# A fused adaLN, dilated-attention and token-MLP kernel: folding a modulation into weights, moving transposes and sums between engines, and issuing in a new order

## The chip, the cores and the metric

The kernel runs on one core of one Trainium2 chip. The metric is device time in microseconds (us) of one execution; less is better. The profiled execution is a little shorter than a timed one, because its span runs only from the first to the last instruction: 225.9 us of span go with 227.8 us of time.

The engines are TensorE (PE in the profile; PEld is its weight load), VectorE (DVE), ScalarE (ACT), GpSimd (POOL) and SyncE (SP; SPq is its queue, which issues nearly all DMAs in order). PSUM is where TensorE writes its results.

## The reference, cut to what matters

```python
# x: (1, 2048, 512); 32 heads of 16; window of 8 keys, dilation 2; MLP of width 1792 over the tokens
mod = silu(c) @ w_mod                       # sa, ca, ga, sb, cb, gb: six rows of 512
h = layernorm(x) * (1 + ca) + sa            # "first modulation"
q, k, v = split(h @ wqkv)
x = x + ga * (dilated_local_attention(q, k, v) @ wo)
h = layernorm(x) * (1 + cb) + sb
h3 = layernorm(h)                           # h3: 2048 tokens x 512
u = gelu(einsum('sd,sf->df', h3, w1) + b1)  # MLP 1 sums over all 2048 tokens
y = einsum('df,fs->ds', u, w2) + b2         # MLP 2
x = x + gb * y.T
```

## The kernel before

The 16 tiles of 128 tokens are worked in five chunks of 2, 4, 4, 4 and 2 tiles. For each chunk: layernorm, transpose, QKV, windowed attention, output projection, two more layernorms to h3. MLP 1 needs all tokens; it is summed in three levels (tiles 0 to 5, 6 to 9, 10 to 15). Between levels the partial sums are "parked" in SBUF as `gT`, and TensorE injects them into the next level's PSUM accumulation with an identity matmul.

Every operation is handed to a small planner in the kernel. It holds a duration for each operation, a rank (RANK, by kind of operation) and a bias between VectorE and ScalarE (BIAS), lays the operations out in time greedily, and thereby fixes both the engine and the order in which each engine gets its instructions. On the chip this order is static.

```python
RANK = {'st1': -69.27, 'ln1': -327.95, 'tr': -152.8, ...}       # order constants
BIAS = {'n1': 1.63, 'hT': 2.81, 'ev': 1.88, ...}
... POOLN1=(3, 5, 7, 8, 11),      # tiles whose first norm runs on GpSimd
    LN2D=(2, 3, 10, 11, 12, 14, 15),  # tiles whose statistics run on VectorE
    NPRE=5,                       # MLP-1 accumulators of the last level begun early
    XDMA=(1, 2, 3, 4),            # chunks transposed by DMA
...
if ch in XDMA:
    for sl, st in enumerate(tiles):
        ... nc.sync.dma_start_transpose(out=hT[:, :, sl * P:(sl + 1) * P], in_=h3[:, st, :])
    for kt in range(KT):          # then the first modulation, in place
        ... tensor_scalar / activation(h_, h_, scale=a1col[:, kt], bias=sacol[:, kt])
else:                             # chunk 0: TensorE transposes, modulation on eviction from PSUM
    ...
# QKV: lhsT = w_r[t][:, kt, j::4], rhs = hT[:, kt, :]
...
# shifted V for the attention: 16 DMAs per chunk on the same queue
dma(dst, v_c[dhi::4, :, s0:s0 + C + 8], ..., f"vd{ch}_{dhi}{w4}")
...
if li > 0:                        # MLP 1: inject the parked sums
    nc.tensor.matmul(ps(s_), lhsT=ident[:], rhs=gT[:, ft, :], start=True, stop=False)
...
if last:
    nc.scalar.activation(gT[:, ft, :], ps(s_), ACT.Gelu_apprx_tanh, bias=b1col[:, ft:ft + 1])
```

## Time and profile before

| | before |
|---|---|
| time, median of 4 runs | 227.83 us (227.06 to 228.93) |
| span of the profiled run | 225.9 us |
| first 512-column QKV matmul (chunk 1) | 35.5 us |
| last h3 tile ready | 158.1 us |
| first MLP-2 matmul | 174.0 us |

The last three rows are milestones. The last h3 tile is the end of the last VectorE `h<-h,rs,nb` instruction (two merged at 157.41, 0.73 us long). Between it and MLP 2 lies the tail of MLP 1, which needs that tile.

Busy time by stretch, kernel before. The columns are the stretch and its length, busy us (and instructions) of PE, PEld, DVE, ACT and POOL, the granted TensorE clock, the DMA share and GB/s.

```profile
8.00:20.00 12.00, 10.14 (x63) 6.99 (x61) 7.04 (x14) 7.33 (x15) 2.22 (x1) 0.72 1.10 312
20.00:46.00 26.00, 16.66 (x124) 6.72 (x125) 17.74 (x30) 14.95 (x28) 5.64 (x5) 0.80 0.76 151
46.00:98.00 52.00, 49.90 (x403) 23.34 (x410) 49.35 (x47) 47.46 (x106) 0.00 (x0) 1.00 0.90 160
98.00:158.00 60.00, 59.63 (x422) 26.15 (x428) 57.43 (x104) 48.40 (x112) 0.00 (x0) 1.00 0.89 200
158.00:174.00 16.00, 15.89 (x74) 7.28 (x75) 0.15 (x1) 8.98 (x14) 0.00 (x0) 1.00 0.41 109
```

From 46 to 158 us TensorE and VectorE are both over 95% busy. From 20 to 46 us neither is, and the clock is at 0.80. From 158 to 174 us VectorE has almost nothing to do, ScalarE is busy for 9 us, and TensorE is full.

Why the start-up is slow shows in the DMA queue's timeline (start, us, what) of the kernel before:

```profile
18.69 1.30 SPq L191 DMA_TRANSPOSE hT<-h  x1
...
21.59 5.13 SPq L191 DMA_DIRECT2D vD<-v_c  x6
26.82 3.86 SPq L191 DMA_TRANSPOSE hT<-h  x3
30.72 2.56 SPq L191 DMA_DIRECT2D vD<-v_c  x4
```

The four transposes of chunk 1 (one, then three) stand in one queue with the V loads of chunk 0. The issue of the last one ends at 30.7 us; ScalarE modulates from 32.4 us on, and the first QKV matmul of chunk 1 starts at 35.54 us.

```profile
35.54 1.90 PE L191 MATMUL psS<-hT,w_qkv 128*128 128x512 bf16 x4
```

Two groups of the kernel before that the change touches (line, engine, operation, count, then busy us and mean ns, then idle time before them and what ended it):

```profile
L191 DVE TENSOR_TENSOR big<-a2sb,vD 128x4096 bf16<-128x4096 bf16 (+1 forms) x20 | 36.9, 1860 | 6.9 <-DMA vD<-v_c 6.7
...
L191 PE MATMUL psS<-gT,ident 128*128 128x512 bf16 x28 | 10.6, 380 | 0.0
```

VectorE loses 6.7 us waiting for V loads; TensorE makes 28 injection matmuls, of which 14 are in the last level.

### The profile page before, as it was taken

How to read it: one execution, taken by the hardware profiler on the slowest of the kernel's cores; microseconds unless marked ns; L12 is line 12 of the kernel's file. 1: busy time of each engine (PE TensorE's matmuls, PEld its weight loads, DVE VectorE, ACT ScalarE, POOL GpSimd, SP SyncE). 2: the span in 40 equal slices, each digit the busy share in tenths (PEclk: the TensorE clock that was granted, in tenths of full speed). 3: DMA queues.
4: the chain of work that ended last, by engine and by line, in shares of the span. 5: the costliest groups of instructions: out<-in, count | busy, mean ns of one | idle time of the engine just before them, and what ended most of it. 6: DMA issues, size and time to landing. Idle time of an engine off the chain costs nothing.

```text
span 225.9 us, 3720 instructions
## 1 busy us (share of the span) xinstructions
PE 205.7 (91%) x1380; PEld 98.5 (44%) x1402; DVE 157.9 (70%) x236; ACT 131.2 (58%) x279; POOL 11.6 (5%) x35
## 2 busy tenths in 40 slices
PE   7596647879999999989999999999999999999993
PEld 6473212334534543735344333444444444444453
DVE  3278874598998989999999998998000344555444
ACT  3646476487979999999897957984744000000000
POOL 6008140000000000000000000000000000000000
PEclk9769885999999999999999999999999999999999
DMA  6999963496999499499998484896255511011111
GB/s 191 353 311 312 177 114 93 105 340 180 142 140 138 104 150 144 101 206 166 173 216 226 115 222 150 246 303 178 73 150 150 129 46 48 25 46 46 49 46 49
DMA packets 55302, 34.76 MB, mean 154 GB/s; under 512 B 20596, under 2 KB 54772, under 8 KB 55284
## 3 DMA queue, kind: packets, MB, share of 16 engines
q1 hardware_dynamic: 55276, 34.52, 68.8%
q8 instruction: 11, 0.18, 0.4%
q14 instruction: 7, 0.06, 0.1%
q10 hardware_dynamic: 8, 0.00, 0.0%
HBM read 22.03 MB, written 2.10 MB: 107 GB/s over the span
## 4 chain that ended last, share of the span: by engine, by line
PE 61%; DMA 12%; SPq 9%; ACT 8%; DVE 6%; issue 3%; DVEq 0%; ACTq 0%
PE psS L191 58%; SPq L191 9%; DMA gT<-in_w_mod_dram 5%; DVE big L191 5%; DMA vD<-v_c 5%; PE psL L191 2%; ACT hT L191 2%; DMA hT<-h 2%; ACT h L191 2%; ACT xx L191 1%; ACT junk L191 1%; ACT v_c L191 1%; ACT a2sb L191 1%; DVE m L191 1%; DVE st L191 1%
## 5 line engine op out<-in xcount | busy, mean ns | idle before, releaser
L191 PE MATMUL psS<-h,wst 128*128 128x512 bf16 x216 | 53.2, 379 | 0.4
L191 PE MATMUL psS<-hT,w_qkv 128*128 128x512 bf16 (+1 forms) x235 | 50.2, 363 | 1.3 <-ACT hT L191 0.7
L191 PEld LDWEIGHTS <-wst 128*128 128x128 bf16 x308 | 29.7, 98 | 33.1 <-issue 1.5
L191 PEld LDWEIGHTS <-w_qkv 128*128 128x128 bf16 x282 | 31.1, 116 | 27.8 <-issue 9.3
L191 DVE TENSOR_TENSOR big<-a2sb,vD 128x4096 bf16<-128x4096 bf16 (+1 forms) x20 | 36.9, 1860 | 6.9 <-DMA vD<-v_c 6.7
L191 DVE SCALAR_TENSOR_TENSOR h<-psS,bcol,gb_bc 128x512 f32<-128x512 f32 (+1 forms) x17 | 12.2, 719 | 41.3 <-PE psS L191 41.3
L191 DVE TENSOR_TENSOR big<-q_sb,k_c 128x4096 bf16<-128x4096 bf16 (+1 forms) x20 | 36.8, 1857 | 0.5 <-PE psL L191 0.5
L191 DVE BATCH_NORM_STATS2 st<-xx 128x6 f32<-128x512 bf16 x23 | 15.6, 677 | 7.9 <-DMA xx<-in_A_x_dram 7.2
L191 ACT ACTIVATE h<-xx,nb,rs 128x512 bf16<-128x512 bf16 x26 | 19.9, 804 | 0.2 <-DVE nb L191 0.2
L191 PE MATMUL psS<-gT,big 128*128 128x512 bf16 x82 | 18.2, 379 | 0.1
L191 PE MATMUL psS<-woq,o_sb 128*128 128x512 bf16 x60 | 16.3, 380 | 1.2 <-ACT o_sb L191 0.9
L191 PE MATMUL psS<-big,stack 128*32 128x512 bf16 (+1 forms) x160 | 11.0, 354 | 6.4 <-DVE big L191 6.3
L191 PE MATMUL psS<-gT,wst 128*128 128x512 bf16 (+1 forms) x83 | 15.3, 343 | 0.1
L191 PEld LDWEIGHTS <-ident 128*128 128x128 bf16 (+1 forms) x121 | 10.4, 113 | 9.4 <-issue 2.2
L191 PEld LDWEIGHTS <-big 128*128 128x128 bf16 x116 | 9.2, 97 | 11.4 <-DMA big<-in_w_mod_dram 1.2
L191 ACT ACTIVATE gT<-psS,bcol 128x512 bf16<-128x512 f32 x14 | 9.2, 688 | 7.2 <-PE psS L191 7.2
L191 ACT ACTIVATE hT<-hT,sacol,a1col 128x512 bf16<-128x512 bf16 (+1 forms) x16 | 11.1, 756 | 2.9 <-DMA hT<-h 2.9
L191 ACT ACTIVATE k_c<-psS 128x512 bf16<-128x512 f32 x16 | 9.5, 596 | 4.6 <-PE psS L191 4.6
L191 DVE TENSOR_TENSOR h<-h,xx 128x512 bf16<-128x512 f32 (+1 forms) x17 | 11.2, 661 | 0.6
L191 ACT ACTIVATE q_sb<-psS 128x512 bf16<-128x512 f32 x16 | 9.5, 595 | 3.6 <-PE psS L191 3.4
L191 ACT ACTIVATE gT<-psS 128x512 bf16<-128x512 f32 x19 | 10.5, 594 | 1.5 <-PE psS L191 1.4
L191 DVE BATCH_NORM_STATS2 st<-h 128x6 f32<-128x512 bf16 x16 | 10.8, 672 | 0.0
(89 smaller groups left out, 212.2 us busy)
## 6 DMA issues: line engine op xcount, KB each, us to landing
vD<-v_c SPq DMA_DIRECT2D x48, 130.0 KB, 5.2
wst<-in_B_w_dram SPq DMA_DIRECT2D x6, 768.0 KB, 5.0
wst<-in_B_w_dram SPq DMA_DIRECT2D x4, 896.0 KB, 5.5
big<-in_B_w_dram SPq DMA_DIRECT2D x3, 896.0 KB, 5.3
vD<-v_c SPq DMA_DIRECT2D x32, 66.0 KB, 3.3
out_dram<-h SPq DMA_DIRECT2D x15, 128.0 KB, 1.7
w_qkv<-in_A_wqkv_dram SPq DMA_DIRECT2D x3, 512.0 KB, 6.7
xx<-in_A_x_dram SPq DMA_DIRECT2D x3, 512.0 KB, 7.1
```

The source lines that it names most:

```text
L191: r = fn(*a, **k)
```

## The change

The intent, in four parts:

1. **Folding.** `(norm * (1+ca) + sa) @ W` equals `norm @ ((1+ca) * W) + sa @ W`. The weights are scaled once (12 pieces of 128x512), `sa @ W` becomes a bias added when q and v are evicted (for k it cancels in the softmax), and the 20 modulations of the transposed activations go.
2. **Chunk 1 transposed by TensorE** instead of DMA.
3. **The last level's parked sums added by VectorE** into PSUM instead of injected by TensorE; and six instead of five early accumulators (NPRE).
4. **A new issue order**: new RANK and BIAS, other tiles on GpSimd and VectorE, other durations in the planner; and *fillers*, idle identity matmuls that the planner puts into TensorE gaps longer than 0.45 us before 48 us of its plan, to keep the clock up.

The diff, cut to its core:

```diff
-RANK = {'st1': -69.27, 'ln1': -327.95, ...}      # 19 ranks, 11 biases
+RANK = {'st1': -24.42, 'ln1': -184.6, ...}       # all new
-    NPRE=5,
+    NPRE=6,
-    POOLN1=(3, 5, 7, 8, 11),
-    LN2D=(2, 3, 10, 11, 12, 14, 15),
-    GRP=(2, 2, 4, 1, 2),
-    XDMA=(1, 2, 3, 4),
+    POOLN1=(2, 3, 4, 10, 11, 12, 13),
+    LN2D=(2, 3, 10, 11, 12, 13, 14, 15),
+    GRP=(2, 2, 4, 1, 1),
+    XDMA=(2, 3, 4),
+    INJ=(1,),
+    VPOOL=(2, 3),
+    FILL=48.0,
...
+    def scale_w(t):
+        for kt in range(KT):
+            ... w_r[t][:, kt, :] = wraw[t][:, kt, :] * a1col[:, kt]   # VectorE or ScalarE; two on GpSimd
+    # qvb[:, t] = sa @ W for q and v, 16 one-column matmuls each
...
-            for kt in range(KT):
-                ... hT = hT * a1col + sacol
...
+            # q, v: eviction adds qvb as a bias
...
+            if e == "pe" and 0.0 < eng_free.get(e, 0.0) < self.FILL and r - eng_free[e] > 0.45:
+                ... order.append(self.filler(t0_, n_, k_[1]))
...
+                    add("dve", 0.69, lambda ft=ft, s_=s_: nc.vector.tensor_tensor(
+                        ps(s_), ps(s_), gT[:, ft, :], op=ALU.add), reads=[("gT", ft)], writes=[s_], ...)
```

More of the change, by code (lines that the diff above doesn't have):

```diff
@@ L89, in add_any, with filler @@
         return op
+    def filler(self, t, n, k):
+        f = _Op(-1, [("pe", n * 0.06, lambda: self.fill_fn(k, n))], 0.0, "filler", 0, 0.0)
+        f.start, f.end = t, t + n * 0.06
+        f.alloc = f.frees = f.behind = None
+        return f
     def schedule(self):
@@ L107, in pick @@
             return min(((max(f[k], f[k + 1]), k) for k in f if k % 2 == 0 and k + 1 in f), default=None)
+        dep_ready = {}
         def ready_time(o, e):
-            r = 0.0
-            if o.alloc is not None and o.alloc.i is None:
-                r = pick(o.alloc)[0] + self.XLAT
-            for d in o.deps:
-                od = ops[d]
-                if od is o.behind or od.eng == e == "pe":
-                    t = od.start + od.dur
-                else:
-                    t = od.end + self.XLAT
-                if t > r:
-                    r = t
+            r = dep_ready.get((o.idx, e))
+            if r is None:
+                r = 0.0
+                for d in o.deps:
+                    od = ops[d]
+                    if od is o.behind or od.eng == e == "pe":
+                        t = od.start + od.dur
+                    else:
+                        t = od.end + self.XLAT
+                    if t > r:
+                        r = t
+                dep_ready[o.idx, e] = r
+            if o.alloc is not None and o.alloc.i is None:
+                r = max(r, pick(o.alloc)[0] + self.XLAT)
             if o.bytes_:
@@ L148, in schedule @@
             o.start = r
+            if e == "pe" and 0.0 < eng_free.get(e, 0.0) < self.FILL and r - eng_free[e] > 0.45:
+                t0_ = eng_free[e]
+                n_ = int((r - t0_ - 0.25) / 0.06)
+                k_ = min(((f, k) for k, f in free["ps"].items()), default=(1e9, None))
+                if k_[0] + 0.2 < t0_:
+                    order.append(self.filler(t0_, n_, k_[1]))
             if o.alloc is not None:
@@ L237, in _t_mm @@
     return n * (cols / 2400.0 + 0.004)
-RANK = {'st1': -69.27, 'ln1': -327.95, 'tr': -152.8, 'qk_w': 51.55, 'v_w': 88.32, 'vd': 56.52, 'qk': 54.4,
-        'sm': -280.01, 'pv': 119.44, 'wo': 286.24, 'ln2': 35.59, 'aff': 123.88, 'ln3': 64.65, 'mod': 49.12,
-        'ld_x2': -99.25, 'ld_mod': -9.58, 'mlp': 1048.65, 'pre': 3000.0, 'last': 5000.0}
-BIAS = {'n1': 1.63, 'hT': 2.81, 'ev': 1.88, 'halo': 2.21, 'a2': 1.96, 'oev': 0.57, 'x1': 1.99, 'n2': 3.01,
-        'n3': -0.23, 'park': -0.82, 'row': 2.4}
+RANK = {'st1': -24.42, 'ln1': -184.6, 'tr': -140.25, 'qk_w': 53.91, 'v_w': 78.53, 'vd': 149.45, 'qk': 108.09,
+        'sm': -342.67, 'pv': 129.78, 'wo': 334.17, 'ln2': -35.94, 'aff': 219.78, 'ln3': 15.39, 'mod': -61.06,
+        'ld_x2': -184.29, 'ld_mod': -33.96, 'mlp': 904.99, 'pre': 2857.66, 'last': 5184.17}
+BIAS = {'wsc': -0.09, 'n1': 5.48, 'hT': 3.91, 'ev': 3.07, 'halo': 3.23, 'a2': 1.6, 'oev': 1.69, 'x1': 6.58,
+        'n2': 4.08, 'n3': -0.4, 'park': -1.13, 'row': 0.54}
 @with_exitstack
@@ L280 @@
     G.WIN = WIN
+    G.FILL = FILL
     R = dict(RANK, **(R or {}))
@@ L342 @@
     onecol = T([P, 1], F32, "onecol")
-    sacol = T([P, KT], F32, "sacol")
     a1col = T([P, KT], F32, "a1col")
@@ L351 @@
     ecol = T([P, KT], F32, "ecol")
+    sab = T([P, KT], BF, "sab")
+    qvb = T([P, 2, 4], F32, "qvb")
     c_t = T([KT, P], BF, "c_t")
@@ L368, in copy2, with dma @@
                          bias=bias, frees=frees)
-    def dma(out_ap, in_ap, nbytes, reads, writes, name, rate=345e3, **kw):
-        return add("sp", 0.6, lambda: nc.sync.dma_start(*(a() if callable(a) else a for a in (out_ap, in_ap))),
+    def dma(out_ap, in_ap, nbytes, reads, writes, name, rate=345e3, issue=0.5, **kw):
+        return add("sp", issue, lambda: nc.sync.dma_start(*(a() if callable(a) else a for a in (out_ap, in_ap))),
                    reads=reads, writes=writes, name=name, bytes_=nbytes / rate, **kw)
@@ L400, in ln_norm @@
         alts = [("dve", 0.42, lambda: nc.vector.tensor_scalar(dst, src, r_, n_, op0=ALU.mult, op1=ALU.add)),
-                ("act", 0.72, lambda: nc.scalar.activation(dst, src, ACT.Identity, scale=r_, bias=n_))]
+                ("act", 0.8, lambda: nc.scalar.activation(dst, src, ACT.Identity, scale=r_, bias=n_))]
         if pool:
-            alts = [("pool", 0.9, lambda: nc.gpsimd.tensor_scalar(dst, src, r_, n_, op0=ALU.mult, op1=ALU.add))]
+            alts = [("pool", 0.8 if st < 6 else 2.0, lambda: nc.gpsimd.tensor_scalar(dst, src, r_, n_, op0=ALU.mult, op1=ALU.add))]
         G.add_any(alts, reads=reads + [("rs", l, g0), ("nb", l, g0)], writes=writes, name=name, bias=bias)
@@ L414 @@
     dma(wmodA[:, :, 0:D], wmod_view[:, :, 0:D], D * D * 2, [], [("wmodA", 0)], "ld_wmod0", behind=G.ops[-1])
+    wraw = (wst[2][:, 0:KT * D].rearrange("p (k n) -> p k n", k=KT),
+            wst[0][:, 0:KT * D].rearrange("p (k n) -> p k n", k=KT), h2_r[0][:, 0:KT, :])
+    wkey = ([("wst", 2)], [("wst", 0)], [("h2", 0, i) for i in range(MT)])
     def ld_w(t):
-        dma(w_r[t][:], wqkv_view[:, :, t * D:(t + 1) * D], D * D * 2, [], [("w_qkv", t)], f"ld_wqkv{t}")
+        dma(wraw[t], wqkv_view[:, :, t * D:(t + 1) * D], D * D * 2, [], wkey[t], f"ld_wqkv{t}")
+    def scale_w(t):
+        for kt in range(KT):
+            d_, s_, a_ = w_r[t][:, kt, :], wraw[t][:, kt, :], a1col[:, kt:kt + 1]
+            alts = [("dve", 0.3, lambda d_=d_, s_=s_, a_=a_: nc.vector.tensor_scalar_mul(d_, s_, a_)),
+                    ("act", 0.7, lambda d_=d_, s_=s_, a_=a_: nc.scalar.activation(d_, s_, ACT.Identity, scale=a_))]
+            if t == 2 and kt in VPOOL:
+                alts = [("pool", 0.8, lambda d_=d_, s_=s_, a_=a_: nc.gpsimd.tensor_scalar(
+                    d_, s_, a_, 0.0, op0=ALU.mult, op1=ALU.add))]
+            G.add_any(alts, reads=wkey[t] + ["a1col"], writes=[("w_qkv", t, kt)], name=f"wsc{t}_{kt}", bias=B["wsc"])
     def ld_x(ch):
@@ L480, with fill_fn @@
     s_w = _Slot("ps")
+    def fill_fn(k, n):
+        for _ in range(n):
+            nc.tensor.matmul(psS[k][:, 0:P], lhsT=ident[:], rhs=ident[:], start=True, stop=True)
+    G.fill_fn = fill_fn
     def f_warm():
@@ L508, in f_cols2, with f_qvb @@
     def f_cols2():
-        nc.vector.tensor_copy(sacol[:], ps(s_m)[:, 0:KT])
         nc.vector.tensor_scalar_add(a1col[:], ps(s_m)[:, KT:2 * KT], 1.0)
-    add("dve", 0.25, f_cols2, frees=s_m, writes=["sacol", "a1col"], name="modcols_cp")
+        nc.vector.tensor_copy(sab[:], ps(s_m)[:, 0:KT])
+    add("dve", 0.25, f_cols2, frees=s_m, writes=["sab", "a1col"], name="modcols_cp")
+    scale_w(1)
+    scale_w(0)
+    scale_w(2)
+    for i_, t_ in enumerate((0, 2)):
+        s_q = _Slot("ps")
+        def f_qvb(t_=t_, s_q=s_q):
+            for j in range(4):
+                for kt in range(KT):
+                    nc.tensor.matmul(ps(s_q)[:, j:j + 1], lhsT=_ap(wraw[t_][:, kt, j:j + 1], [[4, P]]),
+                                     rhs=sab[:, kt:kt + 1], start=(kt == 0), stop=(kt == KT - 1))
+        add("pe", 0.9, f_qvb, reads=wkey[t_] + ["sab"], alloc=s_q, name=f"qvb{i_}")
+        add("dve", 0.15, lambda i_=i_, s_q=s_q: nc.vector.tensor_copy(qvb[:, i_, :], ps(s_q)[:, 0:4]), frees=s_q,
+            writes=[("qvb", t_)], name=f"qvb_cp{i_}")
     def build_mod_rows():
@@ L583, in build_chunk @@
                                                                          in_=h3[:, st, :])
-                add("sp", 0.6, dma_t, reads=[("n1", st)] + ([("hT_raw", bh)] if sl else []),
+                add("sp", 1.25, dma_t, reads=[("n1", st)] + ([("hT_raw", bh)] if sl else []),
                     writes=[("hTr", ch, sl)] + ([] if sl else [("hT_raw", bh)]), bytes_=P * D * 2 / 260e3, name=f"xt{st}")
-            for kt in range(KT):
-                h_ = hT[:, kt, :]
-                s_, a_ = sacol[:, kt:kt + 1], a1col[:, kt:kt + 1]
-                G.add_any([("dve", 0.15 + 0.00051 * C, lambda h_=h_, s_=s_, a_=a_: nc.vector.tensor_scalar(
-                    h_, h_, a_, s_, op0=ALU.mult, op1=ALU.add)),
-                           ("act", _t_act(C, 1.5), lambda h_=h_, s_=s_, a_=a_: nc.scalar.activation(
-                    h_, h_, ACT.Identity, scale=a_, bias=s_))],
-                    reads=["a1col", "sacol"] + [("hTr", ch, sl) for sl in range(nt)], writes=[("hT", bh, kt)],
-                    name=f"hT{ch}_{kt}", bias=B["hT"])
+            hkeys = [("hTr", ch, sl) for sl in range(nt)]
         else:
@@ L609, in build_chunk @@
                     kt = k0 + k2
-                    src = lambda s_=s_, k2=k2: ps(s_).bitcast(BF)[:, k2 * C:(k2 + 1) * C]
-                    G.add_any([("dve", 0.23 + 0.00058 * C, lambda kt=kt, src=src: nc.vector.tensor_scalar(
-                        hT[:, kt, :], src(), a1col[:, kt:kt + 1], sacol[:, kt:kt + 1], op0=ALU.mult, op1=ALU.add)),
-                               ("act", _t_act(C, 2), lambda kt=kt, src=src: nc.scalar.activation(
-                        hT[:, kt, :], src(), ACT.Identity, scale=a1col[:, kt:kt + 1], bias=sacol[:, kt:kt + 1]))],
-                        reads=["a1col", "sacol"], frees=s_, writes=[("hT", bh, kt)], name=f"hT{ch}_{kt}", bias=B["hT"])
+                    copy2(hT[:, kt, :], lambda s_=s_, k2=k2: ps(s_).bitcast(BF)[:, k2 * C:(k2 + 1) * C], C, True, [],
+                          [("hT", bh, kt)], f"hT{ch}_{kt}", B["hT"], frees=s_)
+            hkeys = [("hT", bh, kt) for kt in range(KT)]
         rk("qk_w")
@@ L639, in build_chunk @@
             add("pe", _t_mm(C, 4) * GQ + (0.02 if C < 512 else 0), f,
-                reads=[("hT", bh, kt) for kt in range(KT)] + [("w_qkv", t), ("hT_raw", bh)], alloc=s_,
+                reads=hkeys + [("w_qkv", t, kt) for kt in range(KT)] + [("hT_raw", bh)], alloc=s_,
                 name=f"qkv{ch}_{t}{j0}")
@@ L643, in build_chunk, with fa, fd @@
             dst = (q_sb[:, js, :], k_c[:, js, PAD:PAD + C], v_c[:, js, PAD:PAD + C])[t]
-            copy2(dst, lambda s_=s_: ps(s_)[:, 0:GQ * C].rearrange("p (j s) -> p j s", j=GQ), GQ * C, False, [],
-                  [(("q", "k", "v")[t], bq, j) for j in range(j0, j0 + GQ)], f"ev{ch}_{t}{j0}", B["ev"], frees=s_)
+            src = lambda s_=s_: ps(s_)[:, 0:GQ * C].rearrange("p (j s) -> p j s", j=GQ)
+            ekeys = [(("q", "k", "v")[t], bq, j) for j in range(j0, j0 + GQ)]
+            if t == 1:
+                copy2(dst, src, GQ * C, False, [], ekeys, f"ev{ch}_{t}{j0}", B["ev"], frees=s_)
+                continue
+            bcols = qvb[:, t // 2, js]
+            def fa(dst=dst, src=src, bcols=bcols):
+                for j in range(GQ):
+                    nc.scalar.activation(dst[:, j, :], src()[:, j, :], ACT.Identity, bias=bcols[:, j:j + 1])
+            def fd(dst=dst, src=src, bcols=bcols):
+                if GQ == 1:
+                    nc.vector.tensor_scalar_add(dst[:, 0, :], src()[:, 0, :], bcols)
+                else:
+                    nc.vector.tensor_tensor(dst, src(), bcols.unsqueeze(2).to_broadcast([P, GQ, C]), op=ALU.add)
+            G.add_any([("act", GQ * _t_act(C, 1), fa), ("dve", _t_tt1(GQ * C), fd)], reads=[("qvb", t)], writes=ekeys,
+                      name=f"ev{ch}_{t}{j0}", bias=B["ev"], frees=s_)
         if ch == 0:
@@ L661, in build_chunk @@
                     [("v", bq, j) for j in range(4)] + [("vhalo", bq)], [("vD", ch, dhi, w4)],
-                    f"vd{ch}_{dhi}{w4}", rate=150e3, **(dict(behind=first) if w4 else dict(alloc=s_)))
+                    f"vd{ch}_{dhi}{w4}", rate=150e3, issue=0.65, **(dict(behind=first) if w4 else dict(alloc=s_)))
                 if w4 == 0:
@@ L858 @@
                 early = last and ft < NPRE and len(steps) > 1
+                if last and not early:
+                    steps = [s_lo]
                 first = True
                 G.pk = float(R["pre"]) if early else pk0
-                if li > 0:
+                inj = li in INJ and not last
+                if inj:
                     add("pe", _t_mm(512), lambda s_=s_, ft=ft: nc.tensor.matmul(
@@ L869, with f @@
                     G.pk = float(R["pre"]) if early and s1 < s_hi else pk0
-                    def f(s_=s_, fl=fl, w1p=w1p, s0=s0, s1=s1, li=li, s_lo=s_lo, s_hi=s_hi):
+                    def f(s_=s_, fl=fl, w1p=w1p, s0=s0, s1=s1, inj=inj, s_lo=s_lo, s_hi=s_hi):
                         for s in range(s0, s1):
                             nc.tensor.matmul(ps(s_), lhsT=w1p[:, s - s_lo, fl * P:(fl + 1) * P], rhs=h3[:, s, :],
-                                             start=(li == 0 and s == s_lo), stop=(s == s_hi - 1))
+                                             start=(not inj and s == s_lo), stop=(s == s_hi - 1))
                     add("pe", _t_mm(512, s1 - s0), f, reads=wkeys + [("h3", s) for s in range(s0, s1)],
@@ L877 @@
                     first = False
+                if li and not inj:
+                    if not last:
+                        add("dve", 0.69, lambda ft=ft, s_=s_: nc.vector.tensor_tensor(
+                            gT[:, ft, :], ps(s_), gT[:, ft, :], op=ALU.add), writes=[("gT", ft), "gT_use"], frees=s_,
+                            name=f"padd{li}_{ft}")
+                        continue
+                    add("dve", 0.69, lambda ft=ft, s_=s_: nc.vector.tensor_tensor(
+                        ps(s_), ps(s_), gT[:, ft, :], op=ALU.add), reads=[("gT", ft)], writes=[s_], name=f"padd{li}_{ft}")
                 if last:
@@ L886 @@
     G.pk = float(R["last"]) + 1000.0
-    homes = ([(w_r[t][:].rearrange("p k n -> p (k n)"), 1, [("w_qkv", t)]) for t in (1, 0, 2)] +
+    homes = ([(w_r[t][:].rearrange("p k n -> p (k n)"), 1, [("w_qkv", t, kt) for kt in range(KT)]) for t in (1, 0, 2)] +
              [(hT_r[i][:], 1, [("hT_raw", i)] + [("hT", i, kt) for kt in range(KT)]) for i in range(NHT)] +
```

## The prediction

> **What bounds the kernel now.** Three regimes, from the busy times by stretch (span 225.9 us).
>
> - 0 to 46 us, start-up. From 20 to 46 us TensorE is busy 16.7 of 26 us at a granted clock of 0.80, VectorE 17.7. The timeline and waits show why: chunk 1's four transposes are DMAs, issued at 18.7 and 26.8 us in one in-order queue (1.25 us issue each); ScalarE then modulates (4 x 0.80 us from 32.4); QKV of chunk 1 starts at 35.5 us. The 16 shifted-V loads of chunk 0 share that queue (0.61 us each), stretch from 21.6 to 42.7 us, and cost VectorE 6.2 us of waiting.
> - 46 to 158 us, saturated: TensorE 109.5, VectorE 106.8 of 112 us.
> - From 158 us (last h3 tile) TensorE alone: 73 MLP-1 matmuls at a pitch of 10.74/49 = 0.219 us, then MLP 2, gapless to 222.5 us.
>
> Both bind together; a gain must shorten both.
>
> **What the change does.**
> 1. *Folding.* Removes 20 modulations on ScalarE (11.1 + 1.9 us by group). Adds 12 weight scalings: VectorE about 0.41 us each (measured on a like tensor_scalar), two on GpSimd 0.8 to 2.8. Biased q/v evictions cost ScalarE 0.09 us more (0.688 against 0.594) for 24 large ones, 0.5 more for 8 halved ones. Net ScalarE minus 5 to 8 us; VectorE plus 3 to 4, mostly in idle time before 12 us. The K weights land near 9.0 us, so first QKV is 0 to 0.5 us later.
> 2. *Chunk 1 by TensorE.* Removes 4 x 1.25 us of queue issue; adds 16 small transposes (about 1 us) and four PSUM copies. QKV of chunk 1 should start at 25 to 28 instead of 35.5 us, the V loads finish near 32 to 35 instead of 42.7. Estimate: of VectorE's 8.3 idle us in 20 to 46 us, 5 to 6 disappear.
> 3. *Fillers* in TensorE gaps before 48 us keep the clock up. The Trainium skill, "TensorE: Matmul & The Clock Gate", section "The HAM clock gate", says an idle window halves the clock; this trace agrees in direction (clock 0.66 in 30 to 40 us, modulation matmuls 0.546 us against 0.379 warm). 1 to 3 us, mostly the same gain as 2.
> 4. *Last parked sums on VectorE.* Removes 14 injection matmuls, 3.1 us of TensorE; 14 adds of about 0.69 us fall where VectorE idles 19 us. With six early accumulators the tail after 158 us falls from 73 to 6x2 + 8x6 = 60 matmuls: 2.8 us.
>
> **On the critical path.** The last h3 tile comes 5 us earlier (6 from start-up, minus 1 for added VectorE work), the tail is 2.8 us shorter: 8 us. Point 219.5 us; range 214 to 225. Faster by over 2% (below 223.2): 0.74; within 2%: 0.22; slower: 0.04.
>
> **What would show each step.** (1) No hT modulations; ScalarE busy lower by 5+ us. (2) First 512-column QKV near 26 us; VectorE's V-load wait below 3 us. (3) Granted clock above 0.9 from 10 to 40 us. (4) 14 injections instead of 28; last h3 tile near 153 us; no gap at the MLP-1/MLP-2 boundary; MLP 2 unchanged, about 48 us.
>
> **What would make it wrong.** GpSimd norms of chunk 1 (three tiles; two took 5.6 us beside VectorE) delay its transposes. Added VectorE work eats the gain while saturated. Six early accumulators hold all six PSUM slots and stall TensorE or evictions. If start-up gains nothing, 3 us remain (about 225).

## The result, and the profile after

The changed kernel takes 218.95 us in the median of 4 runs (218.92 to 220.23); before took 227.83 us beside it. The ratio is 0.9631, 95% interval 0.9592 to 0.9670. Executions over 1.5% slower than the fastest of the same kernel are left out of the means.

| milestone | before | after | won |
|---|---|---|---|
| first 512-column QKV | 35.5 | 27.1 | |
| last h3 tile | 158.1 | 151.3 | 6.8 |
| from there to MLP 2 | 15.8 | 13.4 | 2.5 |
| from there to the end | 51.9 | 52.2 | -0.3 |
| span | 225.9 | 216.9 | 9.0 |

The milestones come from these lines of the timeline, first of the kernel before, then of the changed one: the last h3 instructions on VectorE and the first MLP-2 matmuls on TensorE.

```profile
157.41 0.73 DVE L191 TENSOR_SCALAR h<-h,rs,nb 128x512 bf16<-128x512 bf16 x2
173.97 9.23 PE L191 MATMUL psS<-gT,w_qkv 128*128 128x512 bf16 x41
```

```profile
150.90 0.41 DVE L208 TENSOR_SCALAR h<-h,rs,nb 128x512 bf16<-128x512 bf16 x1
164.68 9.23 PE L208 MATMUL psS<-gT,w_qkv 128*128 128x512 bf16 x41
```

Busy time by stretch, changed kernel, columns as above:

```profile
8.00:20.00 12.00, 7.51 (x98) 6.81 (x94) 9.57 (x25) 6.70 (x17) 3.00 (x3) 1.00 1.10 319
20.00:46.00 26.00, 22.72 (x210) 10.87 (x215) 22.92 (x31) 19.29 (x42) 13.90 (x5) 1.00 0.57 165
46.00:98.00 52.00, 49.38 (x398) 24.04 (x403) 50.69 (x55) 44.98 (x102) 5.25 (x3) 1.00 1.17 157
98.00:158.00 60.00, 58.58 (x405) 25.12 (x406) 56.50 (x107) 46.89 (x107) 0.00 (x0) 1.00 0.81 193
```

VectorE does 5.2 us more in 20 to 46 us and 2.5 us more in 8 to 20 us, and stays full afterwards. The clock is 1.00 in all four stretches.

The queue of the changed kernel in the same stretch, and the start of chunk 1 on TensorE:

```profile
20.96 10.68 SPq L208 DMA_DIRECT2D vD<-v_c  x11
32.06 1.31 SPq L208 DMA_TRANSPOSE hT<-h  x1
33.42 2.57 SPq L208 DMA_DIRECT2D vD<-v_c  x4
```

```profile
24.88 0.96 PE L208 MATMUL psS<-ident,h 128*128 128x128 bf16 x14 [2.66 <-POOL h L208]
27.09 1.03 PE L208 MATMUL psS<-hT,w_qkv 128*128 128x512 bf16 x4
```

No transpose stands among the first V loads; chunk 1 is transposed by TensorE as soon as GpSimd has delivered its norm (the wait named in brackets), and its QKV starts 8.4 us earlier than before. The groups that answer to those of before:

```profile
L208 DVE TENSOR_TENSOR big<-a2sb,vD 128x4096 bf16<-128x4096 bf16 (+1 forms) x20 | 36.8, 1860 | 0.2
...
L208 PE MATMUL psS<-gT,ident 128*128 128x512 bf16 x14 | 5.3, 381 | 0.1
...
L208 DVE TENSOR_TENSOR psS<-psS,gT 128x512 f32<-128x512 f32 x14 | 9.2, 696 | 5.1 <-PE psS L208 5.1
```

The V-load wait is gone, 14 injections remain, and 14 adds stand on VectorE where it used to be idle.

### The profile page after: what moved, and what is told of

The parts are those of the page before. It is cut to its first block, busy times and chain, and to the rows that moved or that the text cites. A ratio compares the mean times of both kernels' runs of the same rounds, so it can differ in the third digit from the quotient of the medians.

```text
span 216.9 us, 3882 instructions
## 1 busy us (share of the span) xinstructions
PE 199.7 (92%) x1450; PEld 99.4 (46%) x1474; DVE 170.1 (78%) x264; ACT 125.9 (58%) x276; POOL 25.9 (12%) x39
## 4 chain that ended last, share of the span: by engine, by line
PE 50%; DMA 14%; issue 8%; POOL 8%; SPq 6%; DVE 6%; ACT 4%; POOLq 2%; ACTq 0%
PE psS L208 50%; POOL h L208 7%; DMA vD<-v_c 7%; SPq L208 6%; DMA h<-in_A_wqkv_dram 5%; DVE big L208 3%; DMA wst<-in_B_w_dram 3%; POOLq L1028 2%; DVE h L208 2%; DVE st L208 1%; ACT junk L208 1%; ACT h L208 1%; ACT k_c L208 0%; ACT o_sb L208 0%; DVE mv L208 0%
## 5 line engine op out<-in xcount | busy, mean ns | idle before, releaser
L208 PE MATMUL psS<-h,wst 128*128 128x512 bf16 x216 | 51.5, 379 | 1.4 <-DMA wst<-in_B_w_dram 0.9
L208 PE MATMUL psS<-hT,w_qkv 128*128 128x512 bf16 (+1 forms) x233 | 44.9, 337 | 0.4
L208 PEld LDWEIGHTS <-w_qkv 128*128 128x128 bf16 x282 | 29.6, 112 | 21.0 <-issue 3.8
L208 DVE TENSOR_TENSOR big<-q_sb,k_c 128x4096 bf16<-128x4096 bf16 (+1 forms) x20 | 37.6, 1894 | 0.5 <-PE psL L208 0.5
L208 POOL TENSOR_SCALAR h<-xx,rs,nb 128x512 bf16<-128x512 bf16 x7 | 20.7, 2968 | 14.6 <-DVE nb L208 14.6
L208 PEld LDWEIGHTS <-ident 128*128 128x128 bf16 (+1 forms) x145 | 11.6, 113 | 7.4 <-issue 1.9
L208 ACT ACTIVATE gT<-psS 128x512 bf16<-128x512 f32 x22 | 12.1, 593 | 2.7 <-PE psS L208 2.7
L208 DVE TENSOR_TENSOR psS<-psS,gT 128x512 f32<-128x512 f32 x14 | 9.2, 696 | 5.1 <-PE psS L208 5.1
L208 ACT ACTIVATE q_sb<-psS,qvb 128x512 bf16<-128x512 f32 (+1 forms) x20 | 11.7, 607 | 1.2 <-PE psS L208 1.2
L208 ACT ACTIVATE v_c<-psS,qvb 128x512 bf16<-128x512 f32 (+1 forms) x20 | 11.2, 619 | 1.0 <-PE psS L208 0.8
```

Of the source, the lines that this page charges most:

```text
L208: r = fn(*a, **k)
```

## The experiments

Twelve kernels were run, in four groups; each group shared its runs of the kernel before (median 227.5 to 228.1 us). The question was which of the four parts made the two gains, 6.8 us before the last h3 tile and 2.5 us after it.

| run | time, us | ratio to before (95%) | first QKV | last h3 | tail |
|---|---|---|---|---|---|
| changed kernel | 218.95 | 0.9631 (0.9592 to 0.9670) | 27.1 | 151.3 | 13.4 |
| a_nofill | 219.85 | 0.9652 (0.9608 to 0.9696) | 23.9 | 152.6 | 13.4 |
| a_inj | 222.26 | 0.9778 (0.9726 to 0.9831) | 29.0 | 153.5 | 16.4 |
| a_x1dma | 228.32 | 1.0020 (0.9970 to 1.0069) | 35.0 | 161.1 | 13.4 |
| a_unfold | 227.70 | 1.0016 (0.9952 to 1.0079) | 26.8 | 160.5 | 12.8 |
| b_padd | 224.98 | 0.9841 (0.9774 to 0.9908) | 35.9 | 159.7 | 12.8 |
| b_fill | 229.27 | 1.0057 (1.0005 to 1.0109) | 36.0 | 159.2 | 15.8 |
| a_oldorder | 228.98 | 1.0012 (0.9929 to 1.0096) | 31.0 | 160.7 | 14.5 |
| x1dma_t | 222.72 | 0.9814 (0.9738 to 0.9889) | 34.0 | 155.8 | 12.9 |
| unfold_t | 219.25 | 0.9648 (0.9603 to 0.9692) | 27.2 | 152.8 | 12.8 |
| ux1_t | 225.06 | 0.9913 (0.9854 to 0.9973) | 35.0 | 157.2 | 13.3 |
| acal2 | 221.02 | 0.9655 (0.9610 to 0.9701) | 32.1 | 154.4 | 13.0 |
| after3 | 224.33 | 0.9832 (0.9787 to 0.9877) | 29.2 | 156.6 | 13.4 |

Last h3 is the end of the last h3 instruction on either engine; tail is the time from there to the first MLP-2 matmul, each from the profiled run. All kernels gave correct results. The first row was measured by itself, not in one of the groups.

### Group 1: undo one part, keep everything else

**a_nofill**, fillers off:

```diff
-    FILL=48.0,
+    FILL=0.0,
```

> The changed kernel without the filler matmuls (limit of filling 48 -> 0), nothing else touched. My theory (start-up gain is chunk 1 leaving the DMA queue): 0 to 2 us lost, 219 to 221 us, although the granted clock before 40 us falls back to 0.7 to 0.9. Rival, clock: the fillers hold the clock at full speed and that is most of the 6.8 us by which the last h3 tile moved: 4 us or more lost, 223 us or more, last h3 tile later than 155 us.

Measured 219.85 us; the interval of its ratio overlaps that of the changed kernel. The clock from 8 to 20 us fell to 0.73, and from 20 to 46 us it stayed at 1.00 without any filler, because real work filled TensorE. The rival that the fillers carry 4 us or more falls for the changed kernel; what a cold clock from 20 to 46 us would cost it, this run does not show.

**a_inj**, the last level injected by TensorE again:

```diff
-    INJ=(1,),
+    INJ=(1, 2),
-                inj = li in INJ and not last
+                inj = li in INJ
```

> The changed kernel with the last level's parked sums injected by TensorE again (14 matmuls, no adds on VectorE). My theory: the tail after the last h3 tile grows by 14 x 0.216 = 3.0 us less what the six early injections hide: 1.7 to 3.0 us lost, 220.7 to 222 us, last h3 tile unmoved at 151 +-1 us. Rival: the adds delay gelu and the MLP-1/MLP-2 boundary as much as the matmuls cost: within 0.7 us of the changed kernel.

Measured 222.26 us, 3.3 us lost. The tail grew from 13.4 to 16.4 us, which is 14 x 0.216 us. The last h3 tile came 2.2 us later, more than expected, although the order of instructions on VectorE, ScalarE, GpSimd and the DMA queue is the same up to there (read from the two traces). The profiled execution happened to be the slowest of the four (223.88 us, mean clock 0.969; the others took 221.9 to 222.5 us at 0.982 to 0.984), with a clock of 0.72 and 0.87 in the two start-up stretches where the changed kernel had 1.00. So executions of one kernel differ by 1 to 2 us, here with the lowest mean clock in the slowest. This is no rule: of `a_nofill`'s executions the one of 218.89 us had a mean clock of 0.975, that of 220.05 us one of 0.984. Median against median, the injections cost about the 3 us that the tail shows. First the last h3 instruction, then the first MLP-2 matmul of a_inj:

```profile
153.10 0.41 DVE L208 TENSOR_SCALAR h<-h,rs,nb 128x512 bf16<-128x512 bf16 x1
169.90 9.23 PE L208 MATMUL psS<-gT,w_qkv 128*128 128x512 bf16 x42
```

**a_x1dma**, chunk 1 transposed by DMA again:

```diff
-    XDMA=(2, 3, 4),
+    XDMA=(1, 2, 3, 4),
```

> The changed kernel with chunk 1 transposed by DMA again, folding, fillers and order kept. My theory: first 512-column QKV moves from 27 to about 33 us, V loads of chunk 0 finish 3 us or more later, last h3 tile 3 to 5 us later: 222 to 224 us. Rival, order or folding did it: under 1.5 us lost, below 220.5 us.

Measured 228.32 us: the whole gain was gone, more than my theory could explain. The first QKV came at 35.0 us, some 2 us later than expected; but most of the loss arose later. Busy time of a_x1dma in the stretch that is full in both kernels:

```profile
46.00:98.00 52.00, 47.53 (x409) 23.47 (x407) 43.45 (x38) 37.88 (x81) 0.00 (x0) 1.00 1.17 159
```

VectorE was idle for 8.6 us of the 52, in the changed kernel for 1.3.

**a_unfold**, the folding undone, with the old code for weights, hT and evictions:

```diff
-        dma(wraw[t], wqkv_view[:, :, t * D:(t + 1) * D], D * D * 2, [], wkey[t], f"ld_wqkv{t}")
-    def scale_w(t): ...
+        dma(w_r[t][:], wqkv_view[:, :, t * D:(t + 1) * D], D * D * 2, [], [("w_qkv", t)], f"ld_wqkv{t}")
...
+                ... hT = hT * a1col + sacol, in place or on eviction
-                ... eviction of q and v with bias
+                ... eviction without bias
```

> The changed kernel with the folding undone: weights loaded as they are, hT modulated (16 in place by ScalarE or VectorE after the transposes, 4 + 4 on eviction from PSUM), q and v evicted without bias. ScalarE busy 5 us more, VectorE 3 to 4 us less. My theory: folding is worth little by itself, 0.5 to 2.5 us lost, 219.5 to 221.5 us. Rival, folding: relief of ScalarE in the saturated stretch is the main gain: 4 us or more lost, 223 us or more.

Measured 227.70 us: again the whole gain, although the first QKV came at 26.8 us, as early as in the changed kernel. It matched the rival's number, but so did a_x1dma, and two parts cannot each carry all of it alone. The losses of the four single undos (0.9, 3.3, 9.4 and 8.8 us) add up to 22.3 us, for a gain of 8.9. VectorE was idle 5.9 us between 46 and 98 us here, too. Besides, the TensorE clock was at 0.51 from 93.0 to 103.5 us of this profile, after gaps between its matmuls, well past the time that the fillers cover; what that cost was not tested. (The engines' totals moved less than I had expected, ScalarE by 2.4 us up and VectorE by 0.3 down, because the new plan shared out other work differently.) A new theory was needed: the order constants were chosen for one set of operations, and when one part is undone the planner lays out the rest badly.

### Group 2: add one part to before, and the parts without the order

**b_padd**, the kernel before with VectorE's adds alone:

```diff
-                if li > 0:
+                inj = li > 0 and not last
+                if inj:
                     ... identity matmul
+                if last:
+                    add("dve", 0.69, lambda ft=ft, s_=s_: nc.vector.tensor_tensor(
+                        ps(s_), ps(s_), gT[:, ft, :], op=ALU.add), ...)
```

> The kernel before with one part of the change alone: the last level's 14 parked sums added on VectorE instead of injected by TensorE. My theory: 14 x 0.216 us of TensorE work leave the tail after the last h3 tile, in which nothing else runs: 2 to 3.3 us won, 224.5 to 226 us, last h3 tile unmoved at 158 us. Rival (part of what a_inj lost was its perturbed start-up, whose clock was 0.72 and 0.87 instead of 1.00): under 1.2 us won.

Measured 224.98 us, 2.9 us below before of the same group (227.87). The tail fell from 15.8 to 12.8 us. So this part is worth about 3 us in both surroundings. (The profiled execution was again the slowest of the four, 226.49 us; its last h3 tile came 1.5 us later than in the kernel before.) NPRE stayed at 5 here and at 6 in a_inj, so the sixth early accumulator was not tested by itself. Over all the kernels, the three that inject the last level have tails of 15.8 to 16.4 us, the eleven that add on VectorE 12.8 to 14.5 us.

**b_fill**, the kernel before with the fillers alone:

```diff
+            if e == "pe" and 0.0 < eng_free.get(e, 0.0) < self.FILL and r - eng_free[e] > 0.45:
+                ... order.append(self.filler(t0_, n_, k_[1]))
```

> The kernel before with the fillers alone (same code, filling up to 48 us). My theory: the clock before 46 us rises to 0.9 or more, but the waits there are for DMA and for VectorE, so 0 to 1.5 us won, 226 to 228 us. Rival, clock: the cold clock cost start-up 3 us or more: below 225 us.

Measured 229.27 us; the interval of the ratio lies just above 1. It did raise the clock, from 0.72 and 0.80 to 0.86 and 0.93:

```profile
8.00:20.00 12.00, 10.71 (x116) 9.63 (x116) 6.96 (x14) 7.51 (x16) 2.58 (x1) 0.86 1.10 315
20.00:46.00 26.00, 20.38 (x228) 11.99 (x221) 17.62 (x30) 14.74 (x28) 5.32 (x5) 0.93 0.75 153
```

VectorE's busy time in 20 to 46 us is what it was (17.62 against 17.74 us) and the first QKV came no earlier (36.0 us). TensorE was warmer, and waited for the same things. The clock rival falls for the kernel before as well.

**a_oldorder**, all operations of the changed kernel, order constants of before:

```diff
-RANK = {'st1': -24.42, ...}; BIAS = {...}
+RANK = {'st1': -69.27, ...}; BIAS = {'wsc': -0.09, ... as before}
-    POOLN1=(2, 3, 4, 10, 11, 12, 13),
-    LN2D=(2, 3, 10, 11, 12, 13, 14, 15),
-    GRP=(2, 2, 4, 1, 1),
+    POOLN1=(3, 5, 7, 8, 11),
+    LN2D=(2, 3, 10, 11, 12, 14, 15),
+    GRP=(2, 2, 4, 1, 2),
```

> The changed kernel's operations with the order constants of before (ranks, biases, which norms go to GpSimd, which statistics to VectorE, group sizes). After a_x1dma and a_unfold each lost the whole gain while VectorE lost 5 to 8 us of its busy time between 46 and 98 us, the theory is that the constants are tuned to one set of operations and cost 4 us or more on any other: 223 us or more here. Rival, the parts themselves need each other (both are needed to bring chunk 1 forward): below 221.5 us here, since all parts are present.

Measured 228.98 us over four executions, one of them slow; the three fast ones took 226.96, 227.85 and 230.10 us, and the last of these is the profiled one. The planner's new durations stay in this run. All parts are there, chunk 1 starts at 31.0 us, and nothing is won. So the order is not a detail: with ill-fitting constants the parts are worth nothing together, though the tail alone is 1.3 us shorter than before. Before the last h3 tile VectorE was busy 138.6 us and idle 22.1 us; in the changed kernel it was busy 137.4 and idle 13.9. Busy time up to the last h3 tile, a_oldorder and then the changed kernel:

```profile
0.00:160.70 160.70, 146.06 (x1181) 72.85 (x1182) 138.59 (x213) 118.08 (x262) 16.18 (x37) 0.97 0.84 178
```

```profile
0.00:151.31 151.31, 138.12 (x1157) 70.17 (x1176) 137.42 (x216) 116.12 (x262) 25.91 (x39) 1.00 0.94 194
```

### Group 3: undo one part and fit the order to what remains

If the constants belong to a set of operations, a fair test of a part fits them anew. I searched RANK, BIAS, POOLN1, LN2D and GRP for each set with the kernel's own planner as the yardstick, and ran the best plan on the chip. The planner's times were used only to choose; they are not results.

**x1dma_t**, the operations of a_x1dma:

```diff
-RANK = {'st1': -24.42, ...}; BIAS = {...}
+RANK = {'st1': -91.12, ...}; BIAS = {...}
-    POOLN1=(2, 3, 4, 10, 11, 12, 13),
-    LN2D=(2, 3, 10, 11, 12, 13, 14, 15),
+    POOLN1=(2, 3, 4, 7, 9, 11, 12, 13, 15),
+    LN2D=(11, 12, 13, 14),
```

> The operations of a_x1dma (chunk 1 transposed by DMA, all else as in the changed kernel), but with the order constants searched anew for this set with the kernel's own planner. If the loss of 9.4 us in a_x1dma was mostly a misfitting order, the time falls to 220 to 223 us: TensorE transposes of chunk 1 are then worth 1 to 4 us. If chunk 1's place on TensorE itself is worth the 9 us, it stays at 225 us or more.

Measured 222.72 us: 5.6 us of a_x1dma's loss came back with an order alone, 3.8 us of it stayed. The first QKV of chunk 1 still waits for a transpose, although in this order all four transposes are issued before the first V load. So standing behind V loads is not the whole of the delay:

```profile
24.25 6.64 SPq L208 DMA_TRANSPOSE hT<-h  x3
30.99 3.36 SPq L208 DMA_DIRECT2D vD<-v_c  x5
```

```profile
33.96 6.16 PE L208 MATMUL psS<-hT,w_qkv 128*128 128x512 bf16 x20 [2.14 <-DMA hT<-h]
155.34 0.41 DVE L208 TENSOR_SCALAR h<-h,rs,nb 128x512 bf16<-128x512 bf16 x1
```

**unfold_t**, the operations of a_unfold:

```diff
-RANK = {'st1': -24.42, ...}; BIAS = {...}
+RANK = {'st1': 30.83, ...}; BIAS = {...}
-    POOLN1=(2, 3, 4, 10, 11, 12, 13),
-    LN2D=(2, 3, 10, 11, 12, 13, 14, 15),
-    GRP=(2, 2, 4, 1, 1),
+    POOLN1=(2, 7, 9, 12, 13, 14),
+    LN2D=(2, 3, 4, 10, 11, 12, 13, 15),
+    GRP=(2, 1, 4, 2, 1),
```

> The operations of a_unfold (no folding, all else as in the changed kernel) with the order constants searched anew for this set. If the loss of 8.8 us in a_unfold was a misfitting order: 218 to 222 us, folding worth 3 us at most. If folding itself is worth it: 225 us or more.

Measured 219.25 us, the same as the changed kernel within the intervals, without any folding. One order found suffices to show that folding is not needed for the gain.

```profile
27.23 1.03 PE L208 MATMUL psS<-hT,w_qkv 128*128 128x512 bf16 x4
152.34 0.41 DVE L208 TENSOR_SCALAR h<-h,rs,nb 128x512 bf16<-128x512 bf16 x1
```

Up to its last h3 tile VectorE was busy 132.6 us there, 4.8 us less than in the changed kernel, and idle 20.2 us: having less to do on VectorE did not end it earlier.

**ux1_t**, both undone:

```diff
-    XDMA=(2, 3, 4),
+    XDMA=(1, 2, 3, 4),
... and the folding undone as in a_unfold
-RANK = {'st1': -24.42, ...}; BIAS = {...}
+RANK = {'st1': 375.7, ...}; BIAS = {...}
+    POOLN1=(5, 6, 7, 8, 9, 10, 12, 13, 14), LN2D=(3, 4, 12, 13), GRP=(1, 1, 4, 2, 2),
```

> Folding and chunk 1's TensorE transposes both undone (adds on VectorE and fillers stay), order constants searched anew for this set by the same search with the same budget. If the two parts together carry the start-up gain: 223 to 227 us, last h3 tile at 155 us or later. If the new order alone, on the operations of before, could have brought it: 221.5 us or below. This searched order sends 9 norms to GpSimd, of which each takes 2 to 3.6 us on the chip; if those stall chunk loads, the result only bounds the search and says nothing of the parts.

Measured 225.06 us, which is what b_padd took: without chunk 1 on TensorE and without folding, the best order found gave little at the start: the first QKV came at 35.0 us, the last h3 tile at 157.2 us, 0.9 us earlier than before. In 20 to 46 us VectorE was busy for 22.81 us here, as long as in the changed kernel (22.92), so a full VectorE in that stretch is not by itself the gain.

### Group 4: an attempt to beat both, and its control

**acal2**, GpSimd norms planned near the durations seen on the chip, order searched anew:

```diff
-            alts = [("pool", 0.8 if st < 6 else 2.0, ...
+            alts = [("pool", 2.0 if st < 6 else 3.4, ...
-    POOLN1=(2, 3, 4, 10, 11, 12, 13), LN2D=(2, 3, 10, 11, 12, 13, 14, 15), GRP=(2, 2, 4, 1, 1), XDMA=(2, 3, 4), VPOOL=(2, 3)
+    POOLN1=(2, 6, 9, 10, 12, 13), LN2D=(2, 3, 8, 9, 10, 11, 12, 13, 15), GRP=(2, 2, 2, 4, 1), XDMA=(2, 3), VPOOL=(0, 1, 2, 3)
 ... RANK and BIAS new
```

> An attempt to beat both kernels: the changed kernel's operations, with GpSimd norms planned at the 2.0 and 3.4 us that the trace shows beside VectorE instead of 0.8 and 2.0, and the order constants (and which chunks are transposed by DMA) searched anew. The planner puts the changed kernel at 212.6 with these durations and this one at 209.1. If GpSimd's slow norms cost the changed kernel something: 216 to 218.5 us. If they were hidden behind VectorE anyway: 218.5 to 222 us.

**after3**, its control with the planner's durations left alone:

```diff
-    POOLN1=(2, 3, 4, 10, 11, 12, 13), LN2D=(2, 3, 10, 11, 12, 13, 14, 15), GRP=(2, 2, 4, 1, 1), VPOOL=(2, 3)
+    POOLN1=(3, 4, 9, 12, 15), LN2D=(12, 13, 15), GRP=(2, 2, 4, 2, 1), VPOOL=(0, 1, 2)
 ... RANK and BIAS new
```

> Control for acal2: the same search on the changed kernel's operations with the durations of the change as they are (planner 208.97 against 209.37 of the changed kernel). How well the planner ranks orders at this level is unknown: I expect 218 to 222.5 us, no better than the changed kernel; the distance to it measures how much an equally good plan can differ on the chip.

acal2 took 221.02 us and after3 224.33 us; neither beats the changed kernel. after3 fell outside my expectation: the planner had it level with the changed kernel (208.97 against 209.37), and on the chip it was 5.4 us slower. The loss lies once more in the full stretch, where VectorE was idle 7.3 us of 52. First the busy time of after3 there, then its longest wait on VectorE in the same stretch (us in total, times, longest):

```profile
46.00:98.00 52.00, 46.66 (x373) 21.80 (x378) 44.72 (x44) 38.74 (x92) 0.00 (x0) 0.97 1.01 147
```

```profile
DVE big L208 <- DMA vD<-v_c: 6.3, 4, 3.1
```

This is the wait for V loads that the changed kernel had lost; here it is back, with chunk 1 on TensorE.

This sets the grain of group 3: plans that the planner calls equal can differ by 5 us on the chip. What a good result shows (unfold_t reaches 219.25 us) stands; what a poor one shows (x1dma_t, ux1_t) is only that no better order was found. For the operations of the changed kernel itself the search found 224.33 us, which is more than the 222.72 us that it found with chunk 1 by DMA.

## Why the prediction was right or wrong

The time was predicted at 219.5 us (214 to 225) and measured at 218.95; the split was 5 us before the last h3 tile and 2.8 us after it, measured 6.8 and 2.5. Point by point:

- **Adds on VectorE (item 4): right, mechanism and size; the sixth accumulator was not tested apart.** Predicted 3.1 us of TensorE and a tail 2.8 us shorter; the tail shrank by 2.5 us, grew by 3.0 us when this was undone (a_inj), and shrank by 3.0 us when it alone was done (b_padd). The matmul pitch in the tail is what the Trainium skill, "TensorE: Matmul & The Clock Gate", section "Back-to-back issue gap", gives as the isolated gap (about 216 ns at 512 columns); here 49 matmuls took 10.74 us, which is 0.219 us each.
- **Chunk 1 on TensorE (item 2): the earlier start is shown; how much of the gain is owed to it is not settled.** First QKV at 27.1 us, predicted 25 to 28. In all six versions with chunk 1 by DMA (before included) it came at 34.0 to 36.0 us; in all eight with TensorE at 23.9 to 32.1 us. An early start is not enough: a_unfold has it at 26.8 us and takes 227.70 us. VectorE's idle time in 20 to 46 us fell by 5.2 us, predicted 5 to 6, but in ux1_t, with chunk 1 by DMA, it fell by 5.1 us too. The best orders known differ by 3.8 us beside folding (222.72 against 218.95) and by 5.8 us without it (225.06 against 219.25). Both lie near the grain of 5 us, and the search that found 222.72 us did worse on the changed kernel's own operations, so these differences are no measured worth of the part.
- **V loads (in item 2): wrong in detail.** I said that they finish near 32 to 35 us. The last was issued at 39.97 us, because chunk 2's transposes moved up into the gap. VectorE's wait was gone all the same (0.2 us before that group). I had put this down to chunk 1 leaving the queue; but before 46 us that wait is gone in a_x1dma and x1dma_t as well, which transpose chunk 1 by DMA, and it is 6.2 us in the kernel before. The order of VectorE's work can remove it alone.
- **Fillers (item 3): sized too high.** I gave 1 to 3 us, mostly shared with item 2. The clock went to 1.00 as predicted, but the fillers are worth 0.9 us in the changed kernel, with overlapping intervals, and nothing on the kernel before. The Trainium skill, "TensorE: Matmul & The Clock Gate", section "The HAM clock gate", says that an idle window halves the clock and activity restores it; the trace agrees in direction (from 0.80 to 0.93 in 20 to 46 us when the kernel before got fillers). What I had missed is that a warm clock buys little where TensorE waits. That it buys something at all is not excluded: a_inj's profiled execution, with a colder start and the same order on the other engines, had its last h3 tile 2.2 us later than the changed kernel.
- **Folding (item 1): the total forecast rightly, worth nothing beside chunk 1 on TensorE.** ScalarE's busy time fell by 5.3 us (131.2 to 125.9), predicted 5 or more; but undoing the folding raised it by only 2.4 us in a_unfold and 3.6 us in unfold_t, so part of the fall may have come from the new sharing-out of work. I left it off the critical path, and unfold_t agrees. Without unfold_t the single undo would have said the opposite. With chunk 1 by DMA the searched orders differ by 2.3 us in favour of folding (225.06 against 222.72), inside the grain of the search.
- **The order: missed.** The prediction costs operations and takes for granted that the new set will be laid out as tightly as the old. a_oldorder shows that this is where the gain can be lost entirely: the same operations with the old constants take 227.85 us in the median of the fast executions. The gain was predicted from idle time that the parts could free; the order decides whether VectorE is full between 46 us and the last h3 tile, and so whether the freed time reaches the end. The predicted number came out because the new constants fit the new operations, which I had not examined; in that respect it was luck.

What stays open: why the planner does not foresee the 6 to 9 us for which particular orders leave VectorE idle between 46 and 98 us. The traces show different waits there: 6.3 of 7.3 us for V loads in after3, 4.5 of 5.9 us for ScalarE to deliver q in a_unfold, and no single one in a_x1dma (2.3 us at most of 8.6). Open as well is whether some order would bring the DMA version of chunk 1 to 219 us, and with it how much of the 6.8 us before the last h3 tile is owed to TensorE's transposes and how much to the order.

## What to carry to other kernels

Where two engines are both full in the middle of a kernel, look for time at the ends: work that can start earlier, and work on the last engine running that an idle one can take. In a statically ordered kernel, undoing one part while keeping an order fitted to the whole measures the order as much as the part; refit the order for each variant, or add parts singly to the old kernel, before calling a part necessary. Before keeping the matmul clock up, see what the matmuls wait for: in b_fill the clock rose from 0.80 to 0.93 and nothing was won.

## What the Trainium skill lacked or had wrong

- "TensorE: Matmul & The Clock Gate", section "Back-to-back issue gap", says that in a real kernel, a stream of weight loads and matmuls sustains about 131 ns per 512-column matmul, and that the 216 ns of the isolated formula over-counts. In this kernel, where each matmul has its own weight load, the sustained pitch was 10.74/49 = 0.219 us with the clock at 1.00 (the end of the last matmul included), so the isolated formula holds and the lower figure does not.
- "GPSIMD Engine Reference", section "Specifications", says that GpSimd shares its SBUF interfaces with VectorE, but gives no size for the contention there. (The page "SBUF — State Buffer", section "Who interferes with whom", does say that the one fully blocks the other for a whole instruction, and mentions slow-downs of 1.5 and 6.8 times.) What is lacking is a figure for a norm like this one beside a stream of products. Here the same 128x512 bf16 tensor_scalar took 0.77 us while VectorE paused (kernel before) and 5.92 us beside VectorE's 128x4096 products (x1dma_t); the four norms of chunk 3 in the changed kernel took 14.34 us together:

```profile
32.92 0.77 POOL L191 TENSOR_SCALAR h<-xx,rs,nb 128x512 bf16<-128x512 bf16 x1 [2.79 <-DVE nb L191]
```

```profile
53.02 5.92 POOL L208 TENSOR_SCALAR h<-xx,rs,nb 128x512 bf16<-128x512 bf16 x1 [3.17 <-DVE nb L208]
```

- "TensorE: Matmul & The Clock Gate", section "Part 4: PE-mode transpose", gives about 390 and 275 ns for a single 128x128 transpose. It has no pitch for a stream of transposes (the page has one for plain matmuls of that size): 14 took 0.96 us here, each lasting 0.22 us, so that their starts lay about 0.057 us apart (an estimate: 0.96 less 0.22, over 13).
